# Two-token rows for q and k, k's block moves on GpSimd, and a set of order offsets in a fused attention and two-MLP kernel

## The chip, the cores and the metric

One core of one Trainium2 chip runs the whole program. The metric is the device time of one execution in microseconds, as the median of the timed runs. TensorE is PE here, VectorE DVE, ScalarE ACT, GpSimd POOL; SyncE (SP) issues the DMAs. Each engine executes its own instructions in the order in which the program issues them, and waits for the others by semaphores.

## The reference: what is computed

Three stages one after the other. First a block-diagonal attention: q, k and v have 8 batches, 8 heads, 576 tokens and 64 numbers per head; each chunk of 64 tokens attends to itself alone.

```
scores = scale * matmul(q_c, k_c.T)          # per chunk of 64 tokens
attn = exp(scores - max); attn = attn / (sum(attn) + 1e-9)
x = matmul(attn, v_c)                        # -> 4608 tokens x 512
h = x @ w_in;   x = relu(h)**2 @ w_out       # first MLP, 512 -> 2048 -> 512
h = x @ w_in2;  g = P(h) / (Q(h) + 1e-6)     # P cubic, Q = 1 + |b0||h| + |b1|h*h
out = g @ w_out2                             # second MLP, same sizes
```

The weights come as float64.

## The kernel before, in words

**Numbers and blocks.** Every large product is made of three matmuls in the fp32r type, since each operand is split in a high and a low part: `mm3` (L465 to L467), each 128x128 times 128x512. The 4608 tokens are nine blocks of 512 (`NB`), the 2048 hidden columns sixteen slices of 128 (`NF`). The first five blocks of the first MLP run as 80 steps, s = 0 to 79: `mm_h(s)`, 12 matmuls into one bank of the pool `h_p` (two banks), `act1(s)`, relu and square on ACT (L580, L581 for s from 60, L587, L588 before), a high part and a low part (`gh`, `gl`, DVE or POOL), and 2.5 steps later `mm_out1(s)`, 12 matmuls that add into four ACC banks; `evac1` copies these out after every sixteenth step, by ACT (c = 0, 2) and DVE (c = 1, 3). A step is 24 matmuls. After these steps a second part works through the rest with precombined operands; it is not touched by the change, but its inputs are prepared beside the steps: `w1q_*` sums, splits and stores products of the weights, `xq_*` those of the blocks of x (both mostly on POOL, with a copy on ACT, `room`), `w2_*` those of the second MLP's weights (`w_words`, `w_join`, `w_split` turn float64 words into fp32r parts on ACT, DVE, POOL).

**Attention.** The tokens are 36 tiles of 128. Those from tile 8 on, to which the change applies, come in groups of two tiles that share one start time, in steps: 13.55, 18.55, 22.55, 26.55 and so on by fours to 58.55, then 62.3 and 66.3. For each group: eight loads (`load_qk`, four pairs of heads, q and k; L638), each of 512 tokens of one head. Each of 32 partitions gets, in the form before, rows of 64 numbers (256 bytes) for tokens r, r + 32, r + 64 and so on. `tr` (L661) transposes the blocks of 32x32 on DVE; `tr_mv` then moves two 32-partition blocks for q and two for k from one tile's place to the other's (ACT, L220, `q<-q` and `k<-k`, 32x512), and `tr_part` (L672, DVE) writes the blocks that became free. After that PE makes the scores of a tile (`mm_s`, L706, 32 matmuls of 64x64, written to `a`), DVE and ACT make the softmax, DVE transposes the result to `at`, ACT moves blocks of that, and one group later PE makes P·V of both tiles (`mm_pv2`, L733, 64 matmuls of 64x64), which takes both banks of `h_p`. From there the result goes out in two halves: as a high part by ACT and a low part by DVE (`x2_hi`, `x2_lo`) for blocks that stay, or raw by ACT (c = 0) and DVE (c = 1) (`x1_raw`) and then to memory, `x1d` (`x1_store`); `xq_load` reads it again.

**What sets the order.** There is no planner at run time. The program collects events, `at(t, function, arguments)`, where t is in steps, adds to t a hand-set offset from the table `MOVED` under the event's name, sorts by time and issues the instructions in that order:

```
def at(t, fn, *args):
    key = fn.__name__ + ":" + ...
    events.append((t + MOVED.get(key, 0.0), len(events), fn, args))
```

So an offset moves an event past others only where their times cross, and it matters per engine queue. With a group's start time t0, the load i of eight is at t0 - 0.55 + `LQ_D` i, the transposes at t0 - 1.5, the moves at t0 - 0.95, the parts at t0 - 0.7, P·V and the first tile's scores at t0, the second tile's 0.5 later. `mm_h(s)` is at s (from 62 on, in half steps), `act1(s)` at s + 0.5, `mm_out1(s)` at s + 2.5; for one step in each group it is placed just behind the group's P·V and scores, at t0 + 0.001.

Of the kernel before, what the change touches and what calls it, by code (L numbers as in the profile page):

```python
# [20 lines left out]
UNIT = 256  # L21
NAT = 6
NP1 = 2
TR_A, TR_M, TR_P, S_ODD, C_ODD, LQ_A, LQ_D = -1.5, -0.95, -0.7, 0.5, 1.1, -0.55, 0.28
W2_EARLY = 4
ATTN = [(22.55, 20), (26.55, 22), (30.55, 12), (34.55, 14), (38.55, 24), (42.55, 26), (46.55, 16), (50.55, 18), (54.55, 28),
        (58.55, 30), (62.3, 32), (66.3, 34)]
# [37 lines left out]
MOVED = {  # L65
# [34 lines left out]


@with_exitstack
def attn_moe_moe_kernel(
# [25 lines left out]
    nc = tc.nc  # L129
# [52 lines left out]
    T = {}  # L182
# [35 lines left out]
    def copy(eng, o, x):  # L218
        if eng is nc.scalar:
            nc.scalar.activation(out=o, in_=x, func=ACTF.Copy)  # L220
        else:
            eng.tensor_copy(out=o, in_=x)
# [376 lines left out]
    def half(i):  # L599
        return slice(64 * i, 64 * i + 64)  # L600

    def runs(t0, n):
        done = 0
        while done < n:
            bb, ss = divmod(t0 + done, S)
            step = min(n - done, S - ss)
            yield done, step, bb, ss
            done += step
# [16 lines left out]
    def load_qk(u, src, nm, hp):  # L625
        stage(nm, u, hp)
        if (nm, "room") not in T:
            T[nm, "room"] = tl("attn", [128, HP * UNIT // 32, 32], F32, nm, f"{nm}0")
        x = T[nm, "room"]
        if hp == 0:  # L630
            if T.get((nm, "readers"), 0):
                raise ValueError("the room is still to be read")
            T[nm, "readers"] = 3 if u else 2
        if u:
            b, i = divmod(NAT + 2 * u, TPB)
            Q = 32 * (2 * (hp % 2) + hp // 2)
            for off, n, bb, ss in runs(b * NB, NB):
                nc.sync.dma_start(  # L638
                    out=x.rearrange("p (t e) d -> p t (e d)", e=2)[Q:Q + 32, off // 32:(off + n) // 32],
                    in_=src[bb, 2 * i + hp, ss:ss + n, :].rearrange("(t r) d -> r t d", r=32))  # L640
            return
        for Q in range(4):
            for off, n, bb, ss in runs(NAT * 128, UNIT):
                nc.sync.dma_start(
                    out=x.rearrange("p (a t) d -> p a t d", a=HP)[32 * Q:32 * Q + 32, hp, off // 32:(off + n) // 32],
                    in_=src[bb, 2 * hp + Q // 2, ss:ss + n, 32 * (Q % 2):32 * (Q % 2) + 32].rearrange("(t r) d -> r t d", r=32))

# [14 lines left out]

    def tr_mv(t, o):
        for Q in (0, 64):
            copy(nc.scalar, T[o, t][Q + 32:Q + 64], T[o, t + 1][Q:Q + 32])
        stage("moved", (t, o), 0)

    def tr_part(t, nm, o):
# [31 lines left out]
    def mm_s(t, key):  # L700
        stage("s", t, 0)
        q_, k_ = T.pop(("q", t)), T.pop(("k", t))
        o = banks(T["aps", key], t - key)
        for p in range(HP):
            for h, c in QUARTERS:
                nc.tensor.matmul(out=o[half(c), h, p], lhsT=q_[half(h), p, half(c)], rhs=k_[half(h), p, half(c)],  # L706
                                 start=True, stop=True)
        T["s", t] = o

    def mm_pv(t, key):  # L710
# [9 lines left out]
    def mm_pv2(*ts):  # L720
        o = [h_bank().rearrange("p (t b i) -> p t b i", t=2, i=64) for _ in range(2)]
        for i, t in enumerate(ts):
            stage("softmax", t, 10 if t < 2 * TPB else 7)
            a_ = T.pop(("a", t))
            if t < 2 * TPB:
                v_ = T.pop(("v", t))
            for p in range(HP):
                for c, h in QUARTERS:
                    if t < 2 * TPB:
                        nc.tensor.matmul(out=o[c][half(h), i, p], lhsT=v_[half(c), 2 * p + h], rhs=a_[h][half(c), p],  # L730
                                         start=True, stop=True)
                    else:
                        nc.tensor.matmul(out=o[c][half(h), i, p], lhsT=T["v", ts[p // 2]][half(c), 4 * (p % 2) + 2 * i + h],  # L733
                                         rhs=a_[h][half(c), :, p], start=True, stop=True)
        T["x2", ts[-1]] = [x[:, 0:len(ts)] for x in o]

    def x2_parts(ts, c):
# [546 lines left out]
    for z, (t0, t) in enumerate(seq):  # L1284
# [17 lines left out]
        if t2 < NTILE:  # L1302
            for j in range(2 * HP):
                src, nm = ((q, "qs"), (k_in, "ks"))[j // 2 % 2]
                at(t0 + (LQ_A if z else 0.6) + LQ_D * (j // 4 * 2 + j % 2) * 2 + LQ_D * (j // 2 % 2), load_qk, (t2 - NAT) // 2, src, nm, j // 4 * 2 + j % 2)
    for j in range(2 * HP):
        src, nm = ((q, "qs"), (k_in, "ks"))[j // HP]
# [5 lines left out]
    for j in range(n_first, 2 * NF):  # L1313
        key = w_keys[j]
        jl = j - (2 * NF - n_late)
        t = -0.6 + 0.5 * (j - n_first) if jl < 0 else t_late + 0.6 * jl
# [26 lines left out]
    for u in range(NF // 2):  # L1343
        at(22.1 + 5.3 * u, w1q_copy, u)
        t = T_W1Q[u]
# [7 lines left out]
    for u in range(W2_EARLY):  # L1353
        t = 24.0 + 12.0 * u
# [13 lines left out]
    for i in range(8):  # L1368
        t = NS1 - 27.4 + 1.7 * i + 0.6 * (i > 0)
# [77 lines left out]
    for m in range(KP):  # L1447
        for u in range(NF // 2):
            for x in UNIT_SEQ:
                x = x if x == "o" else int(x)  # L1450
# [113 lines left out]
    for x in pe_list:  # L1564
        if x[0] == "o":
            n = x[1]
# [3 lines left out]
            src = [(made[b, f], E_LAT)] if s >= NS1 else []  # L1570
# [14 lines left out]
            if N_PRE <= n < J_RAW:  # L1585
                e = job("A", COST["hi"], page, due - 16, op_hi, n, nc.scalar)
# [23 lines left out]
        if x[0] == "p":  # L1610
            _, m, u, p = x
# [51 lines left out]
        u, i = divmod(f, 2)  # L1663
# [88 lines left out]
```

## Time and profile before

| | |
|---|---|
| time, median of 3 runs | 1654.57 us (1648.97 to 1654.64) |
| profiled execution, its own time | 1650.9 us |
| its span | 1649.1 us |
| PE busy | 1592.4 us, 97% |
| ACT, POOL, DVE busy | 1097.6, 1070.5, 1053.2 us |
| DMA | 380,356 packets, 440.08 MB, 267 GB/s over the span |
| packets under 512 bytes | 136,896 |

A busy share is an average over the whole program; the attention groups with the loads of q and k lie between about 80 and 500 us. In the rows, "x n" is a count, and a bracket as [2.80 <-ACT ev L220] is the time for which the engine stood still before the instruction, and the instruction that ended it. The granted clock of PE is given as a share of full speed.

### The profile page before, as it was taken

The page shows a single profiled execution, that of the slowest core. Times are in us where ns is not written, and L with a number is a line of the kernel's source. Part 1 is how long each engine was busy: PE and PEld are TensorE (multiplying, and loading weights), DVE is VectorE, ACT ScalarE, POOL GpSimd, SP SyncE. Part 2 cuts the span into 40 slices and gives each one's busy share as a digit, 9 for nine tenths or more (in the row PEclk, how much of TensorE's full clock was granted, in tenths as well). Part 3 has the DMA queues.
Part 4 walks back from the last instruction along what each step waited for, and adds up shares of the span by engine and source line. Part 5 has one row for each costly group of instructions (what it writes and reads, how often), then busy time and mean ns, then how long its engine had stood idle before and what let it go on. Part 6 is the DMA issues. An engine that isn't in the chain of part 4 may idle for free.

```text
span 1649.1 us, 26183 instructions
## 1 busy us (share of the span) xinstructions
PE 1592.4 (97%) x9069; PEld 1308.0 (79%) x9069; DVE 1053.2 (64%) x1498; ACT 1097.6 (67%) x1796; POOL 1070.5 (65%) x1065
## 2 busy tenths in 40 slices
PE   8989999999788999999999999999999999999998
PEld 7867777878566888888878888888888888888887
DVE  6877877777552333233327788878877888788640
ACT  5855556667565556455557787888788878777651
POOL 3645264638662888487847885888588857565554
PEclk9989999999899999999999999999999999999999
DMA  9845788887899899988899999989998997666644
GB/s 248 238 110 147 202 246 252 252 241 224 253 276 370 281 296 301 357 276 284 289 386 326 318 302 370 299 268 300 364 304 269 299 364 256 202 208 203 198 148 146
DMA packets 380356, 440.08 MB, mean 267 GB/s; under 512 B 136896, under 2 KB 260032, under 8 KB 379200
## 3 DMA queue, kind: packets, MB, share of 16 engines
q1 hardware_dynamic: 380224, 438.40, 83.0%
q8 instruction: 73, 1.20, 0.3%
q14 instruction: 59, 0.48, 0.1%
HBM read 318.77 MB, written 119.54 MB: 266 GB/s over the span
## 4 chain that ended last, share of the span: by engine, by line
PE 71%; DMA 8%; ACT 5%; DVE 5%; SPq 4%; POOL 4%; issue 2%; DVEq 0%; ACTq 0%; POOLq 0%
PE acc L465 13%; PE acc L467 13%; PE acc L466 13%; PE h L465 11%; PE h L467 11%; PE h L466 11%; DMA w2q<-st 2%; SPq L638 2%; DMA w2o<-st 1%; ACT at L220 1%; DMA qs<-in_q_dram 1%; SPq L622 1%; DMA ks<-in_k_dram 1%; SPq L836 1%; DVE wc L267 1%
## 5 line engine op out<-in xcount | busy, mean ns | idle before, releaser
L225 POOL TENSOR_TENSOR gl<-spare,gh 128x512 fp32r<-128x512 f32 x200 | 269.1, 1348 | 103.5 <-ACT gh L220 95.0
L1128 POOL TENSOR_TENSOR t<-t,r 128x512 f32<-128x512 f32 x144 | 188.0, 1306 | 150.5 <-ACT t L1120 144.4
L465 PE MATMUL h<-x,w 128*128 128x512 f32 (+1 forms) x648 | 256.2, 395 | 8.4 <-ACT spare L580 6.5
L466 PE MATMUL h<-x,w 128*128 128x512 f32 (+1 forms) x648 | 252.7, 390 | 0.3 <-DVE x L225 0.3
L467 PE MATMUL h<-x,w 128*128 128x512 f32 (+1 forms) x648 | 252.4, 389 | 0.0
L465 PE MATMUL acc<-gh,w 128*128 128x512 f32 x576 | 230.3, 400 | 10.2 <-ACT ev L220 5.2
L466 PE MATMUL acc<-gl,w 128*128 128x512 f32 x576 | 227.5, 395 | 0.0
L467 PE MATMUL acc<-gh,w 128*128 128x512 f32 x576 | 227.5, 395 | 0.0
L466 PE MATMUL acc<-w,gh 128*128 128x512 f32 x575 | 223.8, 389 | 0.0
L467 PE MATMUL acc<-w,gh 128*128 128x512 f32 x575 | 223.8, 389 | 0.0
L465 PE MATMUL acc<-w,gl 128*128 128x512 f32 x575 | 223.8, 389 | 0.0
L465 PE MATMUL h<-w,w 128*128 128x512 f32 x416 | 162.1, 390 | 5.1 <-DVE h L1104 3.7
L467 PE MATMUL h<-w,w 128*128 128x512 f32 x416 | 162.2, 390 | 0.0
L466 PE MATMUL h<-w,w 128*128 128x512 f32 x416 | 162.1, 390 | 0.0
L225 DVE TENSOR_TENSOR w<-w 128x512 fp32r<-128x512 f32 x64 | 68.1, 1068 | 131.2 <-ACT w L220 130.1
L465 PEld LDWEIGHTS h<-x,w 128*128 128x128 f32 x648 | 122.8, 190 | 35.6 <-ACT spare L580 7.3
L467 PEld LDWEIGHTS h<-x,w 128*128 128x128 f32 x648 | 122.9, 190 | 25.4
L466 PEld LDWEIGHTS h<-x,w 128*128 128x128 f32 x648 | 123.0, 190 | 24.9 <-DVE x L225 0.5
L465 PEld LDWEIGHTS acc<-gh,w 128*128 128x128 f32 x576 | 110.0, 191 | 37.6 <-ACT ev L220 6.5
L467 PEld LDWEIGHTS acc<-gh,w 128*128 128x128 f32 x576 | 110.0, 191 | 23.4
L466 PEld LDWEIGHTS acc<-gl,w 128*128 128x128 f32 x576 | 110.2, 191 | 22.4
L467 PEld LDWEIGHTS acc<-w,gh 128*128 128x128 f32 x575 | 108.0, 188 | 22.4
(178 smaller groups left out, 3420.3 us busy)
## 6 DMA issues: line engine op xcount, KB each, us to landing
w<-w2o SPq DMA_DIRECT2D x144, 512.0 KB, 4.8
w<-w2q SPq DMA_DIRECT2D x256, 256.0 KB, 5.4
w<-w1q SPq DMA_DIRECT2D x112, 256.0 KB, 5.6
x2q<-xroom SPq DMA_DIRECT2D x32, 896.0 KB, 6.5
st<-in_moe_w_in_dram SPq DMA_DIRECT2D x32, 512.0 KB, 5.5
st<-in_moe_w_out_dram SPq DMA_DIRECT2D x32, 512.0 KB, 6.1
w2q<-st SPq DMA_DIRECT2D x32, 512.0 KB, 4.6
w<-w1r SPq DMA_DIRECT2D x64, 256.0 KB, 5.6
```

Source lines behind the costliest of these rows:

```text
L220: nc.scalar.activation(out=o, in_=x, func=ACTF.Copy)
L225: eng.tensor_tensor(out=o, in0=x, in1=hi.bitcast(F32), op=ALU.subtract)
L267: nc.vector.scalar_tensor_tensor(out=c, in0=c, scalar=3, in1=st[:, :, 0], op0=ALU.logical_shift_left, op1=ALU.bitwise_or)
L465: nc.tensor.matmul(out=o, lhsT=al, rhs=bh, start=first and i == 0, stop=False, **kw)
L466: nc.tensor.matmul(out=o, lhsT=ah, rhs=bl, start=False, stop=False, **kw)
L467: nc.tensor.matmul(out=o, lhsT=ah, rhs=bh, start=False, stop=last and i == len(pairs) - 1, **kw)
L622: nc.sync.dma_start(out=x[off:off + n, c], in_=v[bb, h0:h0 + 4, ss:ss + n, :].rearrange("h p d -> p h d"))
L638: nc.sync.dma_start(out=x.rearrange("p (t e) d -> p t (e d)", e=2)[Q:Q + 32, off // 32:(off + n) // 32], in_=src[bb, 2 * i + hp, ss:ss + n ...
L836: nc.sync.dma_start(out=x[:, t], in_={"q": q, "k": k_in, "v": v}[nm][0, 4 * k:4 * k + 4, t0:t0 + 128, :].rearrange("h r d -> r h d"))
L1128: nc.gpsimd.tensor_tensor(out=t, in0=t, in1=T["r", b, f], op=ALU.mult)
```

## The change

The eight loads of a group are issued 0.15 step apart instead of 0.28. In a load, a partition takes two tokens in a row (512 bytes) at a time. As this leaves the tokens of a chunk in another order, the scores read k's 64 columns, and P·V the 64 columns of `at`, in a permuted order for the tiles from 8 on. k's moves in `tr_mv` go to POOL, q's stay on ACT. The table `MOVED` is written on one line, and has new entries; one, `w_join:(0,7,1)`, has another value.

```diff
-TR_A, ..., LQ_A, LQ_D = -1.5, -0.95, -0.7, 0.5, 1.1, -0.55, 0.28
+TR_A, ..., LQ_A, LQ_D = -1.5, -0.95, -0.7, 0.5, 1.1, -0.55, 0.15
 MOVED:
-    "w_join:(0,7,1)": -1.599
+    'w_join:(0,7,1)': -1.165
+    'mm_pv2:8,9': 0.05, 'mm_h:32': 0.05, 'xq_lo:0': 0.6, 'o_lo:1': -0.1, 'mm_out1:4': 0.35,
+    'load_qk:1,ks,3': -0.2, 'mm_out1:8' to 'mm_out1:59': -0.1 (but 17: 0.165, 19: -0.2),
+    'evac1:0,2': -0.1, 'w1q_store:2,0': 0.2, 'xq_hi:2': -1.0, 's_norm:17': -0.2, 'op_hi:4': -0.35,
+    'load_v:18': 0.2, 'act1:67': 1.0, 's_exp:35': -0.2, 'w1q_sum2:0' to '7': 0.1 (4: 0.05),
+    'load_qk:14,qs,2': 0.2, 'xp_load:2,0': -1.0, 'o_hi:3': -0.35, 'i_load:6': 1.0
 load_qk:
                 nc.sync.dma_start(
-                    out=x.rearrange("p (t e) d -> p t (e d)", e=2)[Q:Q + 32, off // 32:(off + n) // 32],
-                    in_=src[bb, 2 * i + hp, ss:ss + n, :].rearrange("(t r) d -> r t d", r=32))
+                    out=x.rearrange("p (a t) d -> p a (t d)", t=4)[Q:Q + 32, off // 64:(off + n) // 64],
+                    in_=src[bb, 2 * i + hp, ss:ss + n, :].rearrange("(a r t) d -> r a (t d)", r=32, t=2))
 tr_mv:
         for Q in (0, 64):
-            copy(nc.scalar, T[o, t][Q + 32:Q + 64], T[o, t + 1][Q:Q + 32])
+            copy(nc.gpsimd if o == "k" else nc.scalar, T[o, t][Q + 32:Q + 64], T[o, t + 1][Q:Q + 32])
 mm_s:
-                nc.tensor.matmul(out=o[half(c), h, p], lhsT=q_[half(h), p, half(c)], rhs=k_[half(h), p, half(c)],
-                                 start=True, stop=True)
+                rhs = k_[half(h), p, half(c)]
+                if t >= NAT + 2:
+                    rhs = rhs.rearrange("d (t r) -> d r t", t=2)
+                nc.tensor.matmul(out=o[half(c), h, p], lhsT=q_[half(h), p, half(c)], rhs=rhs, start=True, stop=True)
 mm_pv2:
-                                         rhs=a_[h][half(c), :, p], start=True, stop=True)
+                                         rhs=a_[h][half(c), :, p].rearrange("k x i -> k i x"), start=True, stop=True)
```

## Rows read from the trace of the kernel before

**Rows 1.** The page's 40 slices of the span: PE's busy share in tenths.

```profile
PE   8989999999788999999999999999999999999998
```

**Rows 2.** Windows: length, busy us of PE, PEld, DVE, ACT, POOL; clock; DMA share; GB/s.

```profile
440.00:450.00 10.00, 3.00 (x95) 2.81 (x96) 6.80 (x10) 7.18 (x12) 6.38 (x10) 0.60 0.77 247
600.00:700.00 100.00, 100.00 (x441) 82.52 (x441) 32.15 (x34) 54.99 (x92) 70.18 (x74) 1.00 0.96 326
```

**Rows 3.** PE's waits by releaser: us in total, times, longest.

```profile
PE h L733 <- ACT spare L580: 10.4, 4, 8.9
PE h L733 <- ACT r L587: 9.6, 7, 2.5
PE h L465 <- ACT spare L580: 6.5, 2, 5.9
PE acc L465 <- ACT ev L220: 5.2, 3, 2.8
PE acc L465 <- POOL w L225: 3.0, 1, 3.0
```

**Rows 4.** Groups of instructions, 80 to 520 us: busy us, mean ns | idle before.

```profile
L220 ACT ACTIVATE k<-k 32x512 f32<-32x512 f32 x28 | 17.6, 628 | 0.7
...
L222 POOL CAST st<-wc 128x512 fp32r<-128x512 f32 x16 | 10.0, 624 | 11.2 <-DVE wc L267 11.2
...
L706 PE MATMUL a<-k,q 64*64 64x64 f32 x928 | 21.3, 225 | 0.1
L733 PE MATMUL h<-at,v 64*64 64x64 f32 x896 | 20.8, 231 | 20.0 <-ACT spare L580 10.4 <-ACT r L587 9.6
```

**Rows 5.** Timeline at 251 us, ACT and PE: start, duration, instruction.

```profile
251.97 1.28 ACT L220 ACTIVATE k<-k 32x512 f32<-32x512 f32 x2
...
253.92 0.53 PE L465 MATMUL acc<-gh,w 128*128 128x512 f32 x1 [2.80 <-ACT ev L220]
```

**Rows 6.** Timeline at 144 us, POOL and DVE.

```profile
143.25 2.52 POOL L287 TENSOR_TENSOR w1r<-w 128x512 f32<-128x512 f32 x2 [2.79 <-DMA w1r<-w1r]
...
145.97 0.69 DVE L222 COPY ev<-acc 128x512 f32<-128x512 f32 x1
```

**Rows 7.** Timeline at 483 us, POOL and PE.

```profile
483.15 1.28 POOL L225 TENSOR_TENSOR ee<-ee 128x512 fp32r<-128x512 f32 x1
...
484.23 0.68 PE L706 MATMUL a<-k,q 64*64 64x64 f32 x31
```

**Rows 8.** Timeline at 199 us, PE and DVE.

```profile
198.52 0.39 PE L467 MATMUL acc<-gh,w 128*128 128x512 f32 x1
...
200.12 0.98 DVE L225 TENSOR_TENSOR gl<-r,gh 128x512 fp32r<-128x512 f32 x1
```

**Rows 9.** Timeline at 176 us, PE and DVE.

```profile
175.42 0.65 PE L706 MATMUL a<-k,q 64*64 64x64 f32 x32
...
176.28 1.29 DVE L225 TENSOR_TENSOR x<-h,x 128x512 fp32r<-128x512 f32 x2
```

**Rows 10.** Timeline 428 to 447 us, SP, POOL, ACT and DVE.

```profile
428.75 0.96 SPq L433 DMA_DIRECT2D room<-x1d  x1
...
435.97 1.58 SPq L638 DMA_DIRECT2D qs<-in_q_dram  x1
...
436.02 1.83 POOL L441 TENSOR_TENSOR room<-room 128x128 f32<-128x128 f32 x4 [7.87 <-DMA room<-x1d]
...
439.77 0.67 ACT L259 ACTIVATE wc<-st 128x512 f32<-128x512 f32 x1 [5.50 <-POOL ee L225]
...
440.89 0.93 ACT L220 ACTIVATE room<-room 128x896 fp32r<-128x896 f32 x1
...
441.14 0.71 DVE L661 STREAM_TRANSPOSE q<-qs 128x512 f32<-128x512 f32 x1 [8.60 <-DMA qs<-in_q_dram]
...
445.68 0.60 ACT L580 ACTIVATE spare<-h 128x512 f32<-128x512 f32 x1
```

**Rows 11.** The page's line on DMA packets.

```profile
DMA packets 380356, 440.08 MB, mean 267 GB/s; under 512 B 136896, under 2 KB 260032, under 8 KB 379200
```

More of the change, by code (lines that the diff above doesn't have):

```diff
@@ L23 @@
 NP1 = 2
-TR_A, TR_M, TR_P, S_ODD, C_ODD, LQ_A, LQ_D = -1.5, -0.95, -0.7, 0.5, 1.1, -0.55, 0.28
+TR_A, TR_M, TR_P, S_ODD, C_ODD, LQ_A, LQ_D = -1.5, -0.95, -0.7, 0.5, 1.1, -0.55, 0.15
 W2_EARLY = 4
@@ L64 @@
     "xh2": 'V', "xh4": 'V'}
-MOVED = {
[34 rows of a table removed]
+MOVED = {'w_words:(0,3,0)': -14.15, 'w_words:(0,0,1)': -13.45, 'w_words:(0,2,0)': -11.949, 'w_load:0,4,0': -11.348, 'w_join:(0,2,0)': -11.648, 'w_load:0,2,1': -11.348, 'w_join:(0,3,0)': -11.847, 'w_load:0,5,0': -10.747, 'w_join:(0,0,1)': -12.246, 'w_load:0,4,1': -13.245, 'w_load:0,6,0': -0.499, 'w_words:(0,1,1)': -0.527, 'w_split:(0,3,0)': -0.202, 'w_join:(0,1,1)': -0.8, 'first:half110': 11.902, 'w_words:(0,4,0)': -0.401, 'act1:1': 0.401, 'load_tok:4,v,v0': 1.799, 'load_qk:0,qs,1': 0.899, 'load_qk:0,qs,2': 0.301, 'w_words:(0,2,1)': -0.236, 'w_split:(0,1,1)': 0.465, 's_exp:4': 0.015, 'w_load:0,5,1': -0.02, 'act1:2': -0.084, 'w_words:(0,5,0)': 0.517, 'w_join:(0,5,0)': 0.201, 'w_join:(0,2,1)': -0.022, 'w_split:(0,5,0)': 0.079, 'a_ps:5': -2.202, 'tr_second:5': 0.597, 'f_tr:4': 0.597, 'f_copy:4,0,0': -0.152, 'w_load:0,7,1': -0.802, 'load_qk:0,qs,3': 1.2, 'f_copy:4,0,1': -0.15, 'w_words:(0,6,0)': 0.149, 'w_words:(0,7,0)': -0.324, 'tr_copy:5,q': 0.602, 'w_split:(0,3,1)': -0.047, 'f_copy:4,1,1': 0.153, 'w_load:0,6,1': 0.068, 'tr_copy:5,k': 0.821, 'load_tok:5,v,v1': 0.497, 'w_join:(0,6,0)': 0.902, 'mm_s:5,5': -0.199, 'w_words:(0,4,1)': 0.597, 'w_join:(0,7,0)': 0.698, 'w_load:0,9,1': -1.239, 'w_split:(0,6,0)': 0.862, 'w_words:(0,5,1)': 0.299, 'w_split:(0,7,0)': 0.501, 'w_load:0,10,0': 0.448, 'w_join:(0,5,1)': -0.001, 's_exp:5': 0.048, 'w_join:(0,4,1)': 0.699, 'w_words:(0,8,0)': 0.1, 'act1:5': 0.001, 'load_qk:0,ks,3': 0.899, 'w_split:(0,4,1)': 0.399, 'w_words:(0,7,1)': -1.2, 'w_join:(0,7,1)': -1.165, 'w_load:0,11,0': 0.662, 'act1:6': -0.154, 'w_load:0,8,1': 1, 'f_tr:5': 0.599, 'w_words:(0,6,1)': 0.551, 'w_load:0,13,0': -0.299, 'w_join:(0,6,1)': 0.201, 'w_load:0,12,0': 0.205, 'w_split:(0,6,1)': -0.048, 'w_load:0,10,1': -1.647, 'w_split:(0,7,1)': -0.546, 'f_copy:5,1,0': 0.549, 'w_words:(0,10,0)': 0.101, 'w_join:(0,10,0)': 0.196, 'tr:6,ks,k': 1.648, 'f_copy:5,1,1': 1.049, 'act1:8': 0.001, 'load_tok:6,v,v0': 1.459, 'w_words:(0,9,1)': -0.39, 'w_split:(0,10,0)': 0.35, 'mm_s:6,6': 0.001, 'tr:7,ks,k': 1.202, 'w_join:(0,8,1)': 0.335, 'mm_s:7,6': 0.6, 'w_split:(0,8,1)': -0.05, 'x2_lo:1,5': 0.752, 'w_join:(0,9,1)': 0.143, 'act1:9': 0.5, 'w_split:(0,12,0)': -0.199, 'w_words:(0,13,0)': 0.102, 'f_copy:6,0,0': -0.45, 'w_load:0,15,0': 0.051, 'w_join:(0,13,0)': -0.249, 'w_words:(0,10,1)': -0.322, 'w_join:(0,10,1)': -0.401, 's_exp:7': -0.05, 'w_split:(0,9,1)': 0.55, 's_norm:7': -0.073, 'w_load:0,11,1': -0.022, 'f_copy:6,1,0': 0.079, 'f_copy:6,1,1': 0.08, 'act1:10': 0.081, 'w_split:(0,13,0)': 0.3, 'w_load:0,12,1': -0.199, 'w_split:(0,10,1)': 0.101, 'f_copy:7,0,0': -0.551, 'w_load:0,13,1': -0.293, 'w_join:(0,15,0)': -0.047, 'w_split:(0,14,0)': 0.349, 'w_load:0,15,1': -1.142, 'f_copy:7,0,1': 0.301, 'f_copy:7,1,0': 0.443, 'f_copy:7,1,1': 0.444, 'w_join:(0,12,1)': -0.248, 'w_words:(0,13,1)': 0.101, 'w_join:(0,13,1)': -0.149, 'w_split:(0,13,1)': 0.601, 'w_words:(0,14,1)': 0.998, 'w_join:(0,14,1)': 0.751, 'w_join:(0,15,1)': 0.252, 'w_split:(0,14,1)': 0.999, 'w_split:(0,15,1)': 0.898, 's_tr:8': 0.85, 's_mv:8': 0.85, 's_tr:9': 1.06, 's_mv:9': 1.06, 'act1:17': 0.799, 'x1_store:34,35': -0.1, 'mm_pv2:8,9': 0.05, 'mm_h:32': 0.05, 'xq_lo:0': 0.6, 'o_lo:1': -0.1, 'mm_out1:4': 0.35, 'load_qk:1,ks,3': -0.2, 'mm_out1:8': -0.1, 'mm_out1:9': -0.1, 'mm_out1:10': -0.1, 'mm_out1:11': -0.1, 'mm_out1:12': -0.1, 'mm_out1:13': -0.1, 'mm_out1:14': -0.1, 'mm_out1:15': -0.1, 'mm_out1:16': -0.1, 'mm_out1:17': 0.165, 'mm_out1:18': -0.1, 'mm_out1:19': -0.2, 'mm_out1:20': -0.1, 'mm_out1:21': -0.1, 'mm_out1:22': -0.1, 'mm_out1:23': -0.1, 'mm_out1:24': -0.1, 'mm_out1:25': -0.1, 'mm_out1:26': -0.1, 'mm_out1:27': -0.1, 'mm_out1:28': -0.1, 'mm_out1:29': -0.1, 'mm_out1:30': -0.1, 'mm_out1:31': -0.1, 'mm_out1:32': -0.1, 'mm_out1:33': -0.1, 'mm_out1:34': -0.1, 'mm_out1:35': -0.1, 'mm_out1:36': -0.1, 'mm_out1:37': -0.1, 'mm_out1:38': -0.1, 'mm_out1:39': -0.1, 'mm_out1:40': -0.1, 'mm_out1:41': -0.1, 'mm_out1:42': -0.1, 'mm_out1:43': -0.1, 'mm_out1:44': -0.1, 'mm_out1:45': -0.1, 'mm_out1:46': -0.1, 'mm_out1:47': -0.1, 'mm_out1:48': -0.1, 'mm_out1:49': -0.1, 'mm_out1:50': -0.1, 'mm_out1:51': -0.1, 'mm_out1:52': -0.1, 'mm_out1:53': -0.1, 'mm_out1:54': -0.1, 'mm_out1:55': -0.1, 'mm_out1:56': -0.1, 'mm_out1:57': -0.1, 'mm_out1:58': -0.1, 'mm_out1:59': -0.1, 'evac1:0,2': -0.1, 'w1q_store:2,0': 0.2, 'xq_hi:2': -1.0, 's_norm:17': -0.2, 'op_hi:4': -0.35, 'load_v:18': 0.2, 'act1:67': 1.0, 's_exp:35': -0.2, 'w1q_sum2:0': 0.1, 'w1q_sum2:1': 0.1, 'w1q_sum2:2': 0.1, 'w1q_sum2:3': 0.1, 'w1q_sum2:4': 0.05, 'w1q_sum2:5': 0.1, 'w1q_sum2:6': 0.1, 'w1q_sum2:7': 0.1, 'load_qk:14,qs,2': 0.2, 'xp_load:2,0': -1.0, 'o_hi:3': -0.35, 'i_load:6': 1.0}
@@ L635, in load_qk @@
             b, i = divmod(NAT + 2 * u, TPB)
-            Q = 32 * (2 * (hp % 2) + hp // 2)
             for off, n, bb, ss in runs(b * NB, NB):
+                Q = 32 * (2 * (hp % 2) + hp // 2)
                 nc.sync.dma_start(
-                    out=x.rearrange("p (t e) d -> p t (e d)", e=2)[Q:Q + 32, off // 32:(off + n) // 32],
-                    in_=src[bb, 2 * i + hp, ss:ss + n, :].rearrange("(t r) d -> r t d", r=32))
+                    out=x.rearrange("p (a t) d -> p a (t d)", t=4)[Q:Q + 32, off // 64:(off + n) // 64],
+                    in_=src[bb, 2 * i + hp, ss:ss + n, :].rearrange("(a r t) d -> r a (t d)", r=32, t=2))
             return
```

34 rows, old and new, of the table MOVED are left out of this document.

## The prediction

> **What bounds the kernel now.** I read the page's slices first, then the stretches by window, then TensorE's waits, then what ends each of them, engine by engine. TensorE (PE) is the bound: its slices stand at 9, with one 7 and a few 8s in the first third [rows 1]. The windows say where its idle time is: from 600 us on PE is 100% busy at a granted clock of 1.00, in the stretch 440:450 it works 3.00 of 10 us at 0.60 [rows 2], that is, partly at the lower of its two levels, 1.2 instead of 2.4 GHz, after it stood still. The attention work, the only thing that the diff touches beside its offsets, ends before 500 us. So no part of the change can move anything after that but by the moment at which it starts, and what is to be had is PE's idle time between 80 and 500 us. The waits of PE name it [rows 3]: 10.4 us for `spare` in front of P·V (L733), 9.6 us in seven pieces for `r` in front of the same line, 6.5 us for `spare` in front of the hidden-layer matmuls, 5.2 us for evacuations `ev` of ACC, 3.0 us for a weight `w`: 34.7 us. Half of that is two places, 8.9 and 5.9 us. A cold clock after the long ones makes it dearer: in 440:450 PE's 3.00 us of work at 0.60 would be 1.8 at full clock, so some 1.2 us there.
>
> The bookkeeping: the profiled execution took 1650.9 us, its span 1649.1 us, 1.8 us lie around it. The three timed runs have their median at 1654.57, 3.7 us above it. The sum is made against 1650.9.
>
> **The change, part by part.**
>
> *k's moves on POOL.* Each of 14 groups has two moves of q and two of k on ScalarE (ACT), 0.63 us each [rows 4]; those of k leave, 1.26 us per group, 17.6 us in all. ACT is no bound, so only the places count where PE waits for an ACT instruction that stands behind k's moves. An example is the ACC evacuation at 251 us: k's moves run 251.97 to 253.25, then `ev`, and PE resumes at 253.92 after 2.80 us [rows 5]. There are three waits for `ev`, 5.2 us in all, and one for `w` of 3.0 us, which also stands behind k's moves [rows 3]. Four times 1.26 would be 5.0 us; the two shorter `ev` waits share 2.4, so the smaller has hardly more than half of 1.26 to give, and I count 4.4. On POOL the trace has no 32x512 copy; the nearest row is a 128x512 cast, 0.62 us [rows 4], so two take 1.25 us; bounds 0.6 (a quarter of the partitions, if that counted) and 2.6 us (twice). What decides is the queue: POOL executes in order, and the k moves now stand behind its other work. At 143.25 us POOL is in two sums until 145.77 [rows 6], so k's moves end at 147.0; DVE's `tr_part` of k must follow, and behind that on DVE stands the evacuation `ev`, now at 145.97 [rows 6]. It comes some 2.2 us later, PE has about 0.7 us of slack there (three matmuls of another ACC tile), so 1.5 us come back. In the last group (66.3) `ee` ends on POOL at 484.43 and k's moves behind it at 485.7; the scores of tile 34 run at 484.23 now [rows 7] and wait 1.5 us. Sum of the part: 4.4 - 1.5 - 1.5 = 1.4 us gained; from 4.4 gained (POOL free in both) to 4 lost (three more groups have a split of w1q ahead of k on POOL; about 2 us each would show).
>
> *mm_out1 0.1 step earlier.* For eleven of the steps in which an attention group starts, this puts the 12 matmuls of mm_out1(S-1) ahead of P·V and of the scores on PE's queue, where they were behind. They need no `r` that is being read, so they cover the seven waits of P·V, 9.6 us [rows 3]. Two prices. First, at 199 us `gl` of that very step ends at 201.10 [rows 8], while the matmuls ahead of it are done at 198.91 [rows 8], so mm_out1 waits 2.2 us there, where P·V waited for 2.5 (the longest of the seven). The other six waits, 7.1 us, go. Second, mm_h(S+1) now follows the scores at once, and P·V has both banks of the h pool: mm_h has to wait until one is evacuated. In the group at 175 us the scores end at 176.07 and the evacuation's DVE half at 177.57 [rows 9]; the first bank, which mm_h needs, is free half of the 1.29 us before that, at 176.9, so PE stands 0.9 us after the scores. Until now the 12 matmuls of mm_out1 lay between. Five groups have this form, 4.5 us; five with a raw evacuation (one instruction for each bank) cost some 0.2 us each, 1.0. Sum: 7.1 - 5.5 = 1.6 us gained; bounds 7.1 gained (evacuations covered) and 3 lost (each raw group 1.1 too).
>
> *Loads of q and k earlier (0.15 for 0.28 step).* The last of a group's eight loads goes to SP's queue 0.91 step earlier, about 5 us, past weight loads, the store and load of x1, and the copies of w1q. This speaks to the stall of 8.9 us [rows 3] that ACT's relu at 445.68 ends: its chain is this relu, behind q's and k's moves, behind DVE's transpose at 441.14, which waited 8.60 us for the qs load issued at 435.97. With the load some 7 us earlier the next limit is ACT's `wc` at 439.77, which waited 5.50 us for POOL's `ee`, and this for the landing of `room<-x1d` at 436.0, issued at 428.75 [rows 10]. That load is one of those which the q/k loads now pass: three q/k loads go ahead of it that were behind, one that was ahead is gone: two more issues of about 0.6 us, 1.2 us later. `wc` and `st` end and `room` is done 2.05 us after `wc` starts [rows 10], then come q's moves, 1.26, and the relu, 0.6: 439.77 + 1.2 + 2.05 + 1.26 + 0.6 = 444.9, against 446.28. So 1.4 us gained of 8.9; 2.6 if x1d's load is not delayed; 9.5 with the lost clock on top if I have that chain wrong; 0 if x1d's load is delayed by the whole 2.8 us that the passing loads take. The second long one (5.9 us) hangs on a POOL chain that waits for a store of weights to land, which the change leaves.
>
> *Two tokens in a row.* 14 x 8 x 512 = 57,344 pieces of 256 bytes become 28,672 of 512; of the 136,896 packets under 512 B [rows 11] 42% go. No DMA ends a wait of PE above 2 us in these stretches, but behind ACT and POOL they do (x1d above). Bounds: 0, and 6 us (a fifth of the 34.7). I take 2, nearer to nothing since the number of bytes and of issues is the same.
>
> *Strided operands.* The two-token order permutes k's columns; the scores read k as `d (t r) -> d r t`, 128 bytes from element to element, and P·V reads its weights with blocks 1 KB apart. No row of before has a moving operand of such a pattern. Scores: 928 recorded matmuls, 21.3 us; P·V 896, 20.8 us [rows 4]: with overlap about 0.65 us for each set of 32 (0.98 for 64 with P·V). Bounds: 0 to a doubling, 28 x 0.65 + 14 x 1.0 = 32 us. I take 0: a matmul of 64 columns starts every 20 ns in such a set while one lasts 225 [rows 4], so its length is hardly that of reading columns, and a slower read lies inside it.
> The Trainium skill speaks against this: "SBUF — State Buffer" (the note on SBUF cachelines) says that accesses which cross to a new 16-byte line each time pay a penalty. By that rule the sum would be that of the third rival below; no run so far shows it.
>
> *The rest.* `xq_hi:2` a whole step earlier stands in front of relu(57) on ACT and waits for POOL, which gives back what P·V's wait at that step (the sixth or seventh of rows 3) would have gained: between the mean of the six, 1.2, and the longest of the seven, 2.5, and I take 2.2, since ACT stands there for one of POOL's sums. `act1:67` later, single loads and stores by 0.1 to 1 step: nothing, hidden by PE's own queue; within 1 us either way.
>
> Sum: 1.4 + 1.6 + 1.4 + 2 - 2.2 = 4.2 us. The clock: with shorter stalls the stretch at 0.60 is shorter; 1 us more. That is 5.2 below 1650.9, 1645.7; the same from the median of the runs is 1649.4. I say 1647.
>
> **Rivals.**
> 1. *The stall before 446 goes wholly, the clock stays up.* For it: the loads are the largest named wait (8.60 of 8.9 us). Against it: `wc` on ACT ended at its own late time. It gives 8 us more than the forecast, and 2 of clock, and if P·V's waits vanish without a price 5.5: 1632 to 1639.
> 2. *Nothing gained.* The waits change places: h banks instead of `r`, POOL instead of ACT. For it: each price above is read from rows; against it: ACT really is freed. 1650 to 1657.
> 3. *The strided reads cost.* Place: each mm_s and P·V from tile 8 on; they lie in PE's own queue, nothing covers them. Price 28 x a + 14 x b; the gain above is eaten from 0.1 us on each of the 42 sets, and the kernel is slower by over 0.5% (1662.8) from 16 us on, 0.4 us on each, half of a doubling. A doubling: 1647 + 32 = 1679. For it: nothing like it in the trace. Against it: the start every 20 ns.
> 4. *POOL late.* k's moves late in ten groups by 1 to 2 us, DVE and with it softmax and evacuations late: 1650 to 1662.
>
> **How the numbers follow.** The forecast (1640 to 1652) 0.46, rival 1 0.20, rival 2 0.15, rival 3 0.11, rival 4 0.08. Half a per cent, 8.3 us, is about what a measurement of this kernel can tell from no change. Faster by over that is under 1646.3: all of rival 1 and half of the forecast, and a last hundredth where rival 2 is off, 0.44. Slower, over 1662.8: most of rival 3, a little of 4 and of the mishaps that none of these names, 0.16. Between them 0.40. The range for 8 in 10, from 1633 to 1662, leaves out the far end of rival 1 and nearly all of rival 3; the likeliest case alone has 1640 to 1652.
>
> **What would show it.** k's moves as POOL rows of about 0.63 us and ACT's `ev` after them earlier; L733 without waits for `r`, L465 `h` with new waits of 0.2 to 0.9 us for the evacuations; a wait at 199 us for `gl`; the stall before 446 us shorter by 1 to 3 us and ended by `wc`, `room` and relu, not by a q/k load; sets of 32 score matmuls still 0.65 us long. I am wrong if these sets grow to over 0.9 us, if the stall before 446 goes altogether, or if PE has new idle time above 3 us behind k's moves.

## The result and the profile after

The changed kernel takes 1662.94 us (median of five runs, 1662.42 to 1664.38), the kernel before 1651.57 beside it: ratio 1.0065, 95% interval 1.0050 to 1.0081. It is slower by 0.65%, 11 us, where 1647 was forecast.

The page of the changed kernel: span, busy time of PE, DMA packets. Its instructions stand 34 lines further up in the code than those of before, a few of them 31 or 32 (L431 is before's L465, L701 its L733, L675 its L706). In the kernels before with offsets alone, P·V is L699 and the scores are L672.

```profile
span 1660.7 us, 26209 instructions
...
PE 1598.1 (96%) x9069; PEld 1309.6 (79%) x9069; DVE 1052.9 (63%) x1498; ACT 1079.8 (65%) x1768; POOL 1089.5 (66%) x1093
...
DMA packets 351683, 440.07 MB, mean 265 GB/s; under 512 B 79552, under 2 KB 231360, under 8 KB 350528
```

The 57,344 small packets are gone [rows 11]; the byte count is the same. The span is 11.6 us longer than before. PE's busy time makes 5.7 us of that (1598.1 against 1592.4); the rest is time in which PE stands still. A window of the changed kernel (columns as in rows 2):

```profile
600.00:700.00 100.00, 100.00 (x443) 82.81 (x442) 29.56 (x33) 56.85 (x94) 74.50 (x81) 1.00 0.93 316
```

From 600 to 700 us PE is 100% busy at full clock, as before [rows 2], so the loss lies ahead of that. I followed it by the start of the same hidden-layer matmul in both timelines. The one after P·V of the group at 26.55 starts at 207.64 before and 207.65 after: nothing is lost so far. Two groups later it is 262.92 and 268.43 (5.5 us late), then 392.77 and 405.36 (12.6), 450.24 and 461.36 (11.1), and from 562 us on the difference is 12.1, from 863 us on 11.6. PE's waits in the changed kernel:

```profile
PE h L701 <- ACT spare L546: 8.2, 4, 6.7
...
PE h L431 <- DVE x L191: 6.1, 6, 1.7
...
PE acc L431 <- DVE ev L188: 3.7, 3, 1.5
PE a L675 <- POOL k L188: 3.6, 6, 1.4
...
PE acc L432 <- DVE gl L191: 2.2, 5, 1.0
PE acc L431 <- DVE gh L188: 2.2, 1, 2.2
...
PE h L701 <- ACT r L553: 1.1, 1, 1.1
```

P·V's 9.6 us for `r` [rows 3] are 1.1 now. In their place stand the x evacuation (6.1), `gl` and `gh` (4.4), POOL's `k` (3.6), `ev` on DVE (3.7). Groups of instructions, 80 to 540 us:

```profile
L675 PE MATMUL a<-k,q 64*64 64x64 f32 x928 | 24.0, 238 | 3.6 <-POOL k L188 3.6
...
L188 POOL COPY k<-k 32x512 f32<-32x512 f32 x28 | 19.1, 681 | 28.1 <-DVE k L627 26.8
...
L638 DVE STREAM_TRANSPOSE k<-ks 32x512 f32<-32x512 f32 x28 | 19.7, 703 | 21.1 <-POOL k L188 20.4
```

A move of k takes POOL 0.68 us, hardly more than ACT's 0.63 [rows 4]; but DVE's part of k now waits 20.4 us for it in sum. The scores from tile 8 on are busy for 24.0 us where they were for 21.3 [rows 4].

### The profile page after: what moved, and what is told of

The parts are those of the page before. It is cut to its first block, busy times and chain, and to the rows that moved or that the text cites. A ratio compares the mean times of both kernels' runs of the same rounds, so it can differ in the third digit from the quotient of the medians.

```text
span 1660.7 us, 26209 instructions
## 1 busy us (share of the span) xinstructions
PE 1598.1 (96%) x9069; PEld 1309.6 (79%) x9069; DVE 1052.9 (63%) x1498; ACT 1079.8 (65%) x1768; POOL 1089.5 (66%) x1093
## 4 chain that ended last, share of the span: by engine, by line
PE 72%; DMA 8%; DVE 6%; POOL 5%; ACT 4%; SPq 4%; issue 2%; DVEq 0%; POOLq 0%; ACTq 0%
PE acc L431 13%; PE acc L432 13%; PE acc L433 13%; PE h L431 11%; PE h L432 10%; PE h L433 10%; DMA w2o<-st 1%; DMA w2q<-st 1%; SPq L604 1%; POOL st L191 1%; PE h L701 1%; DMA w1o<-w 1%; ACT at L186 1%; DMA x<-x1q 1%; DVE gl L191 1%
## 5 line engine op out<-in xcount | busy, mean ns | idle before, releaser
L431 PE MATMUL h<-x,w 128*128 128x512 f32 (+1 forms) x648 | 257.6, 397 | 14.7 <-ACT spare L546 6.5
L431 PE MATMUL acc<-gh,w 128*128 128x512 f32 x576 | 228.5, 397 | 15.0 <-ACT ev L186 5.2
L431 PE MATMUL acc<-w,gl 128*128 128x512 f32 x575 | 223.7, 389 | 0.0
L431 PE MATMUL h<-w,w 128*128 128x512 f32 x416 | 162.1, 390 | 4.6 <-DVE h L1072 2.7
L431 PEld LDWEIGHTS h<-x,w 128*128 128x128 f32 x648 | 123.1, 190 | 43.9 <-ACT spare L546 7.3
L431 PEld LDWEIGHTS acc<-gh,w 128*128 128x128 f32 x576 | 109.4, 190 | 43.4 <-ACT ev L186 6.3
```

The source lines that it names most:

```text
L431: nc.tensor.matmul(out=o, lhsT=al, rhs=bh, start=first and i == 0, stop=False, **kw)
```

## The experiments

A ratio is against the kernel before, measured beside it on the same chip (its median was between 1650.46 and 1652.66), with its 95% interval. Where an edit starts from the kernel before it says "before", else "changed". A trace is of one execution, and executions of the kernel before took from 1645.1 to 1659.8 us; so a single wait that differs by a few us between two traces can be chance, and what a change is worth is read from the ratios.

**k's moves back on ACT (changed).**

```diff
-            copy(nc.gpsimd if o == "k" else nc.scalar, T[o, t][Q + 32:Q + 64], ...
+            copy(nc.scalar, T[o, t][Q + 32:Q + 64], ...
```

> The changed kernel with k's moves back on ACT, all else as changed. Theory P (k's moves stand behind POOL's sums and splits, DVE's part of k waits for them, scores, softmax and evacuations come late; that is most of the 11 us lost): about 1652 us, at most 1655, DVE's k part no longer waits for POOL. Rival O (mm_out1 ahead of P.V takes the cover of mm_h and brings gl late; that is the loss): stays at 1660 or more, the waits of mm_h for the x evacuation (six of 0.9 to 1.7 us) remain. Rival S (strided moving operands cost): stays at 1660, score sets stay longer.

1661.28 us, 1.0048 (1.0030 to 1.0066). My first theory, that POOL's queue is most of the loss, falls: the interval overlaps that of the changed kernel.

**k's moves on POOL alone (before, the same line the other way).**

> The kernel before with k's moves on POOL alone. Theory P: 6 to 12 us slower than before, 1658 to 1664, with DVE's k part waiting about 20 us in sum for POOL. Rivals O and S: within 3 us of before, 1649 to 1655, since POOL is no bound.

1651.35 us, 0.9993 (0.9974 to 1.0013): level. POOL is late where it was foreseen, but it also gives something. PE's waits in this kernel:

```profile
PE h L733 <- ACT r L587: 5.6, 5, 1.7
PE a L706 <- POOL k L222: 4.9, 5, 3.1
PE acc L465 <- DVE ev L222: 4.4, 3, 1.8
...
PE acc L465 <- ACT ev L220: 1.7, 2, 1.2
```

`r` and ACT's `ev` give back 4.0 and 3.5 us against rows 3; `k` and DVE's `ev` take 4.9 and 4.0 (4.4, of which 0.4 were there before).

**The 52 offsets of mm_out1 alone (before).**

```diff
+ "mm_out1:8" to "mm_out1:59": -0.1, (17: 0.165, 19: -0.2)
```

> The kernel before with the 52 offsets of mm_out1 (steps 8 to 59) alone. Rival O: 5 to 10 us slower, 1657 to 1662. Theory P: between 4 us faster and 2 us slower, 1648 to 1654; P.V's 9.6 us of waits for r gone but for one, and waits of 0.9 us for the x evacuation in five groups in their place.

1663.84 us, 1.0064 (1.0042 to 1.0086): the order alone costs as much as the whole change. PE's waits in it:

```profile
PE h L699 <- ACT spare L546: 13.1, 4, 11.6
PE acc L431 <- ACT ev L186: 8.3, 3, 4.5
...
PE h L431 <- DVE x L191: 5.8, 6, 1.0
PE acc L431 <- POOL w L191: 5.4, 3, 2.9
PE acc L432 <- DVE gl L191: 4.5, 5, 1.3
...
PE acc L431 <- DVE gh L188: 3.2, 2, 2.5
```

Two kinds are here. `gl`, `gh`, `x` and `xraw` (2.2 us for 1.1) are direct waits of the moved matmuls and of those behind them: 14.7 us more, where `r` gives back 8.9. But `spare` rose from 8.9 to 11.6 in one place, by 2.7 us, `ev` from 5.2 to 8.3 in sum and the wait for `w` from 3.0 to 5.4 [rows 3]: 8.2 us at places where no offset moved anything. PE's busy time is only 1.3 us longer in this trace (1593.7); the loss is standing still.

**Only the eleven early ones (before).**

```diff
+ "mm_out1:12", "mm_out1:21", "mm_out1:25", ... by fours to "mm_out1:57": -0.04
```

> The kernel before with only the eleven early mm_out1 (steps 12, 21, 25 and so on by fours to 57) 0.04 step earlier, just enough to stand ahead of P.V and the scores; the other 41 unchanged. Theory O (the place of these eleven is the cost): 1660 to 1667, as with all 52 offsets; waits of mm_out1 for gh and gl, of mm_h for the x evacuation, and the stall before 446 us longer by 2.7 us. Rival: the other 41 offsets cost: within 3 us of before.

1661.70 us, 1.0056 (1.0038 to 1.0073): these eleven are the cost, the other 41 can't be told from nothing.

**Only the first tile's scores later (before).**

```diff
+ "mm_s:10,10", "mm_s:20,20", ... (eleven groups): 0.002     # behind mm_out1(S-1); P.V stays
```

> The kernel before with only the first tile's scores of a group (32 matmuls) moved behind mm_out1(S-1); P.V stays where it was. Theory C (the scores start the softmax chain; each place where that chain's end is awaited gets the 2.7 us of these 12 matmuls): 4 to 8 us slower, 1655 to 1660, with longer waits for ev at 251 and 356 us and a longer stall before 446, but no new waits for gl and x. Rival D (the direct waits of mm_out1 for gl and of mm_h for x are all of the 12 us): within 2 us of before.

1666.05 us, 1.0079 (1.0051 to 1.0108), more than either expectation. No matmul waits for `gl` or `gh` in it, none longer for `x` than before, and it is the slowest of all. Timelines of this kernel, PE and ACT, in the group at 26.55:

```profile
203.43 1.98 PE L699 MATMUL h<-at,v 64*64 64x64 f32 x62 [3.49 <-ACT r L553]
205.34 0.79 PE L431 MATMUL acc<-gh,w 128*128 128x512 f32 x1
...
210.31 0.69 PE L672 MATMUL a<-k,q 64*64 64x64 f32 x32
...
212.58 0.63 ACT L761 ACTIVATE e<-e 128x512 f32<-128x512 f32 x1 [6.53 <-DVE e L756]
...
229.02 1.70 ACT L186 ACTIVATE at<-u 32x256 f32<-32x256 f32 x4 [5.46 <-DVE at L780]
```

The scores start at 210.31, about 5 us behind P·V's end, since the twelve matmuls between ran mostly at the lower clock after the 3.49 us of standing (granted clock 0.56 from 205.4 to 210.3). The exponential follows at 212.58, and the moves of `at` for both tiles end at 230.7. Before, these were at 207.24 and 224.8. The moves of q and k and the relu that frees P·V's bank queue behind them on ACT. So PE's waits for `r` grow from 9.6 us to 17.3:

```profile
PE h L699 <- ACT r L553: 17.3, 10, 3.6
```

That is the mechanism in this kernel: the scores start a chain (softmax of two tiles, transposes, `at`, moves, relu, next P·V) that is nearly as long as the four steps beside it. Before, from the end of the scores at 203.4 to the end of the wait at 229.4, it took 26.0 us; from one P·V to the next PE took 28 there. What delays the scores is waited for at the next P·V, and at the evacuations (`ev` 6.8 us for 5.2). Of the 17.9 us that the span is longer, waits make about 8; the rest is busy time (1601.8 us for 1592.4), part of it work at the lower clock behind them. The stall before 446 is not longer here (7.3 for 8.9 us), against the expectation. So its 2.7 us in the kernel with 52 offsets do not come from the scores alone; P·V, which went back with them there and not here, is the other candidate, and no run separates it.

**Scores ahead of P·V (before).**

```diff
+ "mm_pv2:8,9", "mm_pv2:10,11", ... (thirteen groups): 0.0005
```

> The kernel before with the first tile's scores ahead of P.V in every group from 18.55 on. Theory C: the softmax chain starts 0.7 to 2.5 us sooner where P.V waits for r, scores fill that wait: 3 to 8 us faster, 1643 to 1649. Rival D: the 0.65 us of scores hide in seven waits, 3 us at most: 1648 to 1652.

1648.59 us, 0.9978 (0.9958 to 0.9998): slightly faster, inside what either expected; it does not tell them apart. The scores now wait for k's moves on ACT (13.8 us in 12 waits, 8.0 of them before 446 us).

**The changed kernel without the 52 offsets.**

```diff
- 'mm_out1:8' to 'mm_out1:59'
```

> The changed kernel without its 52 offsets of mm_out1 from step 8 to 59. Theory O: back by 9 to 13 us, 1649 to 1654. If the parts overlap (POOL's k moves and the strided reads, 0.09 us per set of 32 scores, cost more together): 1655 to 1660.

1658.44 us, 1.0050 (1.0035 to 1.0064). Not back: 7 us remain, and the gain against the changed kernel (1.0065) is not clear of the intervals. So there is a second cause besides mm_out1's place.

**Only the 27 other offsets (before).**

```diff
+ 'xq_hi:2': -1.0, 'w1q_sum2:0' to '7': 0.1, 'act1:67': 1.0, 'mm_out1:4': 0.35, ... (27 entries)
```

> The kernel before with only the 27 small offsets that are not of mm_out1 8 to 59. If the parts add up (moves on POOL 0, two-token loads with permuted reads +1.5 us, and 7.4 for all but mm_out1's offsets): these must cost about 5 to 6 us, 1656 to 1658. If instead the parts overlap (POOL's moves are late by more when w1q's sums come 0.1 step later and the reads are longer): within 2 us of before.

1648.19 us, 0.9968 (0.9950 to 0.9987): faster, against both expectations, so these aren't it. The two places of `xq_hi:2`, PE's timeline and waits:

```profile
419.25 1.87 PE L699 MATMUL h<-at,v 64*64 64x64 f32 x59 [4.23 <-ACT r L553]
...
PE h L699 <- ACT spare L546: 4.9, 4, 3.2
```

The wait for `r` at 415 us is 4.23, 2.0 more than before; the stall before 446 is 3.2 instead of 8.9. The traced execution is as long as that of before (spans 1649.0 and 1649.1), so it does not show where the gain of the median lies; nor was it separated which of the 27 offsets gives it.

**Without the 52 offsets and with k on ACT (changed).**

```diff
- 'mm_out1:8' to 'mm_out1:59'
-            copy(nc.gpsimd if o == "k" else nc.scalar, ...
+            copy(nc.scalar, ...
```

> The changed kernel without mm_out1's 52 offsets and with k's moves on ACT: two-token loads, 0.15 step, permuted reads and the 27 small offsets. If the parts add up: 1656 to 1660, as with the moves on POOL. If the overlap is of POOL: 1650 to 1654.

1655.60 us, 1.0017 (1.0001 to 1.0034): 0.33% below the one with POOL. With mm_out1 in its old place and the loads 0.15 apart, POOL costs something.

**Two tokens, permuted reads and 0.15 (before).**

```diff
-LQ_D = 0.28   +LQ_D = 0.15
-... "(t r) d -> r t d", r=32     +... "(a r t) d -> r a (t d)", r=32, t=2
+... rhs.rearrange("d (t r) -> d r t", t=2);  a_[h][half(c), :, p].rearrange("k x i -> k i x")
```

> The kernel before with two tokens in a row, the permuted (strided) reads that belong to them, and the loads 0.15 step apart; nothing else. Rival S: 5 us slower or more, sets of 32 score matmuls over 0.75 us and P.V longer. Theory P: 2 to 6 us faster, 1646 to 1650, the stall of 8.9 us before 446 us shorter by 1 to 4 us, scores at most 0.05 us longer per set.

1654.22 us, 1.0009 (0.9991 to 1.0026): level, between the two expectations, and the stall before 446 is 9.4 us in it, not shorter.

**Only the permuted reads (before; the columns come out in another order).**

```diff
+... rhs.rearrange("d (t r) -> d r t", t=2);  a_[h][half(c), :, p].rearrange("k x i -> k i x")
```

> The kernel before with only the permuted reads of k by the scores and of at by P.V (loads as before, so the columns come out in another order). If the strided moving operand has its price in PE's own time (0.09 us per set of 32 scores, about 0.18 us per P.V, as the sets of the changed kernel last 0.78 for 0.69 us): 28 x 0.09 + 14 x 0.18 = 5 us slower, 1655 to 1658. If PE's waits take it up: within 2 us of before.

1654.78 us, 1.0015 (0.9997 to 1.0033), between the two expectations and not clear of no change. The reads do cost PE's own time. A set of scores in this kernel's timeline lasts 0.78 us (L709), where 0.69 stood before (L706); the P·V of the group at 175 us lasts 1.34 us (L735) for 1.16 (L733):

```profile
210.45 0.69 PE L706 MATMUL a<-k,q 64*64 64x64 f32 x32
...
210.69 0.78 PE L709 MATMUL a<-k,q 64*64 64x64 f32 x32
...
174.44 1.16 PE L733 MATMUL h<-at,v 64*64 64x64 f32 x64
...
171.94 1.34 PE L735 MATMUL h<-at,v 64*64 64x64 f32 x64
```

**Only the loads 0.15 apart (before).**

```diff
-LQ_D = 0.28
+LQ_D = 0.15
```

> The kernel before with only the loads 0.15 step apart. If the early loads are what offsets the strided reads in the kernel with both parts (which was level with before): 2 to 5 us faster, 1646 to 1649. If the larger pieces do that: within 2 us of before.

1659.52 us, 1.0051 (1.0032 to 1.0069): 7 to 8 us slower alone, against both expectations. The profiled execution took 1653.55, the shortest of its eight, but the delay shows in it. The first line is of before, the others of this kernel:

```profile
POOL st L401 <- DMA w2q<-st: 38.6, 6, 10.9
...
POOL st L401 <- DMA w2q<-st: 47.5, 7, 12.5
...
ACT wc L259 <- POOL ee L225: 11.6, 4, 5.0
...
PE acc L465 <- ACT ev L220: 11.8, 3, 6.9
```

POOL waits 8.9 us longer for stores of w2q to land, ACT's copy of weight words `wc` waits 11.6 us for POOL's `ee` (one wait of 5.5 before [rows 10]), and PE 11.8 us for `ev` (5.2 before [rows 3]).

**k on POOL and 0.15 (before).** Both edits as above.

> The kernel before with k's moves on POOL and the loads 0.15 step apart. If the two overlap (loads of q and k put w1q's stores and copies back on SP, POOL's chain behind them and k's moves come later): 3 to 6 us slower than before, 1654 to 1657. If not: as each alone, 1648 to 1652, and the 4.6 us between the changed kernel without mm_out1's offsets with k on POOL and on ACT come from the small offsets of w1q's sums or from the permuted reads.

1661.01 us, 1.0064 (1.0044 to 1.0084), slower than either expectation, with 14.0 us of waits for k in the scores (4.9 with POOL's moves alone):

```profile
PE a L706 <- POOL k L222: 14.0, 11, 6.7
```

The slowness against before is about that of the loads alone, so a clear overlap is not shown by the times; by the waits, POOL's part of it is.

**The changed kernel without the 52 offsets and with 0.28 again.**

```diff
- 'mm_out1:8' to 'mm_out1:59'
-LQ_D = 0.15
+LQ_D = 0.28
```

> The changed kernel without mm_out1's 52 offsets and with the loads 0.28 step apart again: k's moves on POOL, two-token loads, permuted reads and the small offsets stay. If the earlier loads are the rest of the loss (alone 6.9 to 8.4 us slower): 1649 to 1654, 5 to 9 below the 1658.4 with 0.15. If POOL's moves and the permuted reads are: 1656 to 1660.

1646.81 us, 0.9970 (0.9956 to 0.9984): from 0.5% slower to 0.3% faster by the spacing alone, and faster than either expectation. This is the second cause. Waits of PE and of POOL with 0.28, then with 0.15:

```profile
PE a L675 <- POOL k L188: 1.5, 4, 0.5
...
POOL st L367 <- DMA w2q<-st: 34.3, 6, 10.1
```

```profile
PE a L675 <- POOL k L188: 9.6, 8, 4.0
...
POOL st L367 <- DMA w2q<-st: 41.8, 6, 11.7
```

And SP and POOL around 210 us, with 0.28, then with 0.15:

```profile
206.77 0.39 SPq L377 DMA_DIRECT2D w2q<-st  x1
207.20 2.06 SPq L604 DMA_DIRECT2D qs<-in_q_dram  x2
...
227.73 1.36 POOL L188 COPY k<-k 32x512 f32<-32x512 f32 x2
```

```profile
205.81 0.92 SPq L604 DMA_DIRECT2D ks<-in_k_dram  x2
206.77 0.91 SPq L604 DMA_DIRECT2D qs<-in_q_dram  x2
...
209.05 0.38 SPq L377 DMA_DIRECT2D w2q<-st  x1
...
212.75 0.74 POOL L367 TENSOR_TENSOR st<-wc 128x256 f32<-128x256 f32 x1 [9.45 <-DMA w2q<-st]
...
229.47 1.27 POOL L188 COPY k<-k 32x512 f32<-32x512 f32 x2
```

More of the q and k loads stand ahead of the store of w2q on SP, the store goes 2.3 us later, POOL waits for its landing (the buffer `st` must be free) and its whole queue with k's moves comes 1.7 us later, although PE was 1.8 us ahead at the P·V of 200 us. In sum POOL waits 7.5 us more for these stores, PE 8.1 us more for k. The kernel is also as fast as the one before with the 27 offsets alone (0.9968): k's moves on POOL, two-token rows and permuted reads together show no price on top of these.

**Two tokens and permuted reads at 0.28 (before).**

> The kernel before with the two-token loads and the permuted reads, 0.28 step apart. The reads cost 2 to 3 us, the larger pieces must give back 6 to 8 in the kernel with 0.15. If they do so here as well: 1645 to 1649. If they only undo what the early loads cost: 1652 to 1656.

1655.83 us, 1.0029 (1.0017 to 1.0041): at the slow end of the second expectation; the larger pieces show no gain. The edit is that of two tokens above without `LQ_D`. With 0.15, POOL waits longer for the stores of w2q here too (45.2 us for 37.6), as with k on POOL alone (44.6 for 35.4). But the kernel with 0.15 is not the slower one here (1.0009), so a late POOL does not always reach PE. Why not in this pair, I can't explain from these traces.

**Three variants meant to be faster (before).** Scores ahead of P·V, with a relu moved ahead on ACT; the same with k on POOL in nine groups; and the scores with the 27 offsets:

```diff
+ 'mm_h:21', 'mm_h:25', ... 'mm_h:57': -0.1;  'act1:21', 'act1:25', ... 'act1:57': -0.58
+ copy(nc.gpsimd if o == "k" and t in (10, 20, 22, 14, 24, 16, 18, 30, 32) else nc.scalar, ...
+ the 27 entries, and 'mm_pv2:...': 0.0005
```

> The kernel before with the first tile's scores ahead of P.V, and in ten steps the relu that stands on ACT behind the moves of at and of weight words put ahead of them, its mm_h 0.1 step earlier (no other PE work is passed). Theory C (the chain scores, softmax, transposes, moves, relu, P.V of a group is about as long as the four steps it lies beside, so that what shortens it shortens the time): 1.2 us of ACT less in the chain of each of ten groups, 3 to 8 us below the kernel with the scores alone, 1641 to 1646. Rival (P.V's own waits are all that counts): as the scores alone, 1648 to 1650.

1651.15 us, 0.9998 (0.9979 to 1.0018): no gain, against what the theory expected: an earlier relu does not shorten what decides.

> The same with k's moves on POOL in the nine groups where POOL has no sum or split of w1q right ahead (not at 13.55, 30.55, 42.55, 54.55 and 66.3). Theory C: the scores no longer wait for q's moves and k's in turn on ACT (1.26 us a group); 2 to 5 us below the one without, 1637 to 1643. Rival (POOL late in those groups too): 1646 or more.

1657.27 us, 1.0043 (1.0029 to 1.0057): slower, as the rival has it; the scores wait 10.8 us for k on POOL.

> The kernel before with the 27 small offsets and the scores ahead of P.V, both of which were faster alone by 2.5 to 3.4 us. If they act at different places: 1644 to 1647. If both shorten the same stall before 446 us: 1647 to 1650.

1645.73 us, 0.9964 (0.9949 to 0.9978): faster than both kernels, not clearly more than the 27 offsets alone.

## Why the prediction was wrong, step by step

- **"mm_out1 0.1 step earlier", 1.6 us gained, bounds 7.1 gained and 3 lost.** This is the first step that failed. Alone it costs 10 to 12 us. The waits for `r` went as foreseen (9.6 to 1.1), and the evacuation of x came as priced (0.87 in the changed kernel, 0.96 alone, for 0.9; the raw ones 0.23 for 0.2). But `gl` and `gh` hold mm_out1 in five groups, 7.7 us in sum with the 52 offsets alone (4.4 in the changed kernel), where I priced one at 2.2: the moved matmuls come sooner in every group, not only there. And I counted only waits of the instructions that change places. P·V and scores also went back by twelve matmuls, and the softmax chain hangs from the scores; moving these alone costs 0.79%. The waits at places where nothing moved (8.2 us with the 52 offsets alone) I had at nothing.
- **"Loads of q and k earlier", 1.4 us gained.** The second step that failed, wrong in sign: alone 1.0051, and with mm_out1 in place 0.15 instead of 0.28 turns 0.9970 into 1.0050. I followed one place where the loads pass something, x1d's load, and not the stores of w2q, for which POOL waited 38.6 us before in 6 waits. At the one place that I worked out the chain held: the stall before 457.45 is 6.73 us (2.1 shorter, 1.4 forecast; 1.3 shorter in the kernel with the spacing alone, where k's moves are still in the chain) and is ended by the chain named there, in the timelines of ACT and PE of the changed kernel:

```profile
453.41 0.68 ACT L225 ACTIVATE wc<-st 128x512 f32<-128x512 f32 x1 [5.53 <-POOL ee L191]
...
454.53 0.94 ACT L186 ACTIVATE room<-room 128x896 fp32r<-128x896 f32 x1
455.50 1.28 ACT L186 ACTIVATE q<-q 32x512 f32<-32x512 f32 x2
456.80 0.60 ACT L546 ACTIVATE spare<-h 128x512 f32<-128x512 f32 x1
...
457.45 0.47 PE L701 MATMUL h<-at,v 64*64 64x64 f32 x2 [6.73 <-ACT spare L546]
```

- **"k's moves on POOL", 1.4 us gained.** Level alone (0.9993), which does not contradict 1.4 us of gain. The parts of the sum were in part off: `ev` on ACT gave back 3.5 us, but the wait for `w`, counted at 1.26, gave none (3.8 for 3.0 with POOL's moves alone). PE's wait for `ev` at 144 us became 0.95 instead of 0.67 (1.5 more foreseen), and the last group's scores waited 0.72 and 0.32 for k (1.5 foreseen). Beside the earlier loads POOL's queue is later, and then it costs. One sign of being wrong came: in the changed kernel PE stands 3.6 us in sum behind k's moves.
- **"Strided operands", 0 taken of 0 to 32.** There is a price: 0.09 us on a set of 0.69, and 1.34 for 1.16 on P·V. 28 x 0.09 + 14 x 0.18 make 5.0 us of PE, by estimate from these rows; alone the time moved by 0.15% (about 2.5 us, the interval just takes in nothing). PE's busy time in the changed kernel, 5.7 us longer, has room for all of it, but it also holds work at the lower clock, and no run parts the two. The argument by starts every 20 ns was wrong in part. The Trainium skill's rule that an access to a new 16-byte line pays a penalty ("SBUF — State Buffer", the note on SBUF cachelines) has the right sign; the doubling that I took as the far bound did not come.
- **"Two tokens in a row", 2 us gained.** No gain shown (1.0029 with the permuted reads that belong to them, 1.0015 for these reads alone).
- **"The rest", 2.2 us lost.** The loss at 415 us was right (2.0 more), but the 27 offsets gain 3.4 us in all. In their trace the stall before 446 is 5.6 us shorter and the waits for `r` 3.4 longer (13.0 for 9.6); that the gain comes from there is not shown.

Rivals: the nearest was the second, "the waits change places", but its price (1650 to 1657) was too low. The slow end was given to the strided reads, which alone cost 0.15%, not to the order or the loads.

What is not settled: the two causes do not add up. mm_out1's place alone costs 0.64%, the spacing alone 0.51%, both in the changed kernel 0.65%; taking out the first leaves 0.50%, taking out both gives 0.30% less than before; the changed kernel with only the spacing undone was not tried. So each of the two is shown to cost by itself, in a kernel without the other, and how the 0.65% divides between them is not. That fits waits in one chain of which the latest counts, but no run shows it.

## What to carry to other kernels

When instructions are moved ahead on an engine, price those that they push back, by following what hangs from these, not only what they wait for: twelve matmuls, 2.7 us, ahead of the 32 small ones from which a chain of softmax starts cost 0.6 to 0.8%. An earlier load is not free on a queue in order: list the stores that it passes and who waits for the buffers behind them. Undoing one part of a change may show little while another part remains (here 0.15%, not clear of the noise); undo them together as well.

## What was not expected of the hardware

A moving operand of 64 columns read 128 bytes apart makes a set of 32 score matmuls of 64x64 13% longer (0.78 for 0.69 us). POOL's copy of 32x512 f32 took 0.68 us in the changed kernel, about as long as its cast of 128x512 there (0.66): a quarter of the partitions did not make it shorter.
